# RWKV-6 attention followed by a GELU MLP: the finest level of the attention matrix, taken from TensorE to VectorE

## The chip, the cores and the metric

The kernel runs on one core of one Trainium2 chip. The metric is the device time in microseconds; lower is better. Times given are the median of three runs and one profiled execution, in which a hardware profiler records every instruction.

## The reference, cut to what matters

The first half is a recurrence over 768 steps for 4 batches and 8 heads of 48 channels; its output, laid out as 3072 tokens of 384, goes through an MLP with an exact GELU.

```python
state = np.zeros((B, H, D, D))
for t in range(S):
    cur = einsum('bhd,bhe->bhde', u * k_t, v_t)
    y[:, :, t] = einsum('bhd,bhde->bhe', r_t, state + cur)
    state = w_t[..., None] * state + einsum('bhd,bhe->bhde', k_t, v_t)
x = y.transpose(0, 2, 1, 3).reshape(3072, 384)
h = x @ w_in                       # 384 -> 2048
out = (0.5 * h * (1 + erf(h / sqrt(2)))) @ w_out      # 2048 -> 384
```

So y at step t is a sum over earlier steps s of v_s, weighted by the sum over channels of r_t times the decays w between s and t times k_s; for s = t the factor u stands in place of the decays.

## The kernel before, in words

The sequence is cut into x = 0 to 7, each one half (384 steps) of one batch, all eight heads. `attention(x, unit)` is a generator that computes one x in slots (each `yield` ends one), and `mlp(x)` a generator that computes the MLP of x in steps. The main loop (L844) runs `mlp(x - 1)` and, after its steps, advances `attention(x)` and the first two slots of `attention(x + 1)` at the step numbers in `place` and `place_next`, and starts loads of x + 1 at the step numbers in `times`. There is no scheduler: each engine executes its instructions in the order in which this code issues them, and only waits for what they read or overwrite. Where an instruction on an engine waits, all that was issued to that engine later waits behind it.

In memory channels are on the 128 partitions (two groups g of 64, one per head of a pair) and r, k and w have 1536 steps in the free dimension: four pairs of heads, 384 steps each, step innermost. They lie in two buffers of 4608 floats: `bufs[1]` holds k and w of every x and r of odd x; r of even x has the first third of `bufs[0]`, and the rest of `bufs[0]` holds small things (`alone`, `p1_alone`, `diag_sb`).

Inside chunks of 64 steps the attention matrix `a_sb` is made by levels. For x >= 2 (`quarters`) the levels are h = 1, 4, 16: at level h a block of 4h steps is cut in four, and products between a later quarter of r and an earlier quarter of k are made, where r and k have been multiplied by the decays up to the quarter's edge. At each level VectorE and ScalarE lay out r in `kx` (`lay_out` L442 and L443, `plain` L437), TensorE makes 48 products of 64x64 by 96 columns (L463, a "burst" of 96 records, since each fp32 product is recorded twice), VectorE multiplies r and k by the decays for the next level (L470, L476, L479) and places the results in `a_sb` with nine masked copies (L494). The diagonal s = t is made on VectorE: r k u (L322), summed over 32 partitions by a transposing reduction (L324), then over groups by four small products with a 0/1 matrix `both` (L456), and copied with a mask (L500).

After h = 16, k is transposed by 32x32 blocks (L416), twelve blocks are moved between partitions by transfers (eight on SP's queue, four on ACT's, L411), four copied by ScalarE (L523); then come kv products (L539), the state (L551 to L558), y from `a_sb` (L571), y from the state (L589), and copies and transfers to `xT`, which the MLP reads (L602, L609).

The slots of attention(x), x >= 2: 1 the diagonal's sums; 2 decay totals (L341) and the layout of h = 1; 3 burst h = 1; 4 burst h = 4; 5 burst h = 16; 6 block moves and copies of h = 16; 7 k blocks copied; 8 kv; 9 state; 10 y; 11 y from the state. x = 0 and 1 use another scheme (`halves`), which the change leaves alone.

Steps of `mlp(x)` for x >= 1: 0 to 15 one product group (L656, 384 columns) and its GELU on ScalarE (L659) each, two PSUM buffers in turn; in the groups at f = 13 and 15 VectorE makes sums and differences for a seven-product scheme (L669 to L671); steps 16 to 22 are its seven products of 16 records (L676); odd x (except the last) have two more, 25 steps in all, and even x five more, 28 in all (L760 to L780). `mlp(0)` has 48 steps: 16 groups, then w_out products (L790) while VectorE still converts w_out.

Of the kernel before, what the change touches and what calls it, by code (L numbers as in the profile page):

```python
# [10 lines left out]
F32 = mybir.dt.float32  # L11
# [3 lines left out]
U8 = mybir.dt.uint8  # L15
# [5 lines left out]
C = 64  # L21
# [8 lines left out]
QUARTERS = (1, 4, 16)  # L30
# [13 lines left out]
def kernel(  # L44
# [58 lines left out]
    diag_sb = bufs[0][:, 3 * ALL - NP * T // 32:]  # L103
# [92 lines left out]
    s_qs = {h: q_ints[0][:, i * C:(i + 1) * C] for i, h in enumerate(QUARTERS)}  # L196
# [24 lines left out]
    m_qs = {}  # L221
    for i, h in enumerate(QUARTERS):
        for a in range(3):
            w_q = (3 - a) * C // 4
            z = q_ints[1 if a == 0 else 2]
            o = i * C if a < 2 else i * C + C // 2
            m_qs[h, a] = z[:, o:o + w_q]
            nc.gpsimd.iota(m_qs[h, a], pattern=[[4, C // 4 // h], [0, (3 - a) * h]], base=a, channel_multiplier=0)

    def make_quarter_masks():  # L230
        for (h, a), m_q in m_qs.items():
            nc.vector.tensor_tensor(out=quarter[h][a], in0=s_qs[h][:, 0:m_q.shape[1]], in1=m_q, op=ALU.is_equal)
# [3 lines left out]


    both = const.tile([128, 2, C], F32, name="both")
    nc.gpsimd.memset(both, 0.0)
    for z in range(4):  # L240
        o = slice(z * 32, (z + 1) * 32)
        for i in range(2):
            nc.gpsimd.tensor_copy(out=both[o, z // 2, i * 32:(i + 1) * 32], in_=ident[o, o])
# [55 lines left out]
    def attention(x, unit):  # L299
# [17 lines left out]

        if x >= 2:

            for q in range(qs):  # L320
                z = slice(q * T, (q + 1) * T)
                nc.vector.scalar_tensor_tensor(out=kx[:, z], in0=r[:, z], scalar=u_sb[:, q:q + 1], in1=k[:, z],  # L322
                                               op0=ALU.mult, op1=ALU.mult)
            nc.vector.tensor_reduce(out=diag_sb, in_=kx[:, 0:n_u].rearrange("p (m j) -> p m j", j=32), axis=mybir.AxisListType.X,  # L324
                                    op=ALU.add, apply_transpose=True)
# [17 lines left out]
        if x < 2:  # L343
            yield
# [75 lines left out]
        def quarters():  # L420
# [24 lines left out]
            plain(1)  # L445
            lay_out(1)
            yield
            for h in QUARTERS:
                m, r4, t4, s0, s1, s2 = views(h)
                banks = [ps.tile([128, 2, BANK], F32, name="d", tag="d", bufs=3) for _ in range(0, np_ * NI, 4)]  # L450
                if h == 1:

                    halves_of = diag_sb.rearrange("p (n c z) -> p n c z", c=2, z=2)
                    for g in range(2):
                        for c in range(2):
                            nc.tensor.matmul(banks[-1][half[c], g, 6 * C:6 * C + 2 * np_ * NI], lhsT=both[:, g, :],  # L456
                                             rhs=halves_of[:, :, c], start=True, stop=True)
# [38 lines left out]
                if h == 1:  # L496
                    data = banks[-1][:, :, 6 * C:6 * C + 2 * np_ * NI].rearrange("p g (n z) -> p g n z", z=2)
                    data = data.unsqueeze(4).to_broadcast([128, 2, np_ * NI, 2, C // 2])
                    mask = masks[0].rearrange("p (z t) -> p z t", z=2).unsqueeze(1).unsqueeze(1)
                    nc.vector.copy_predicated(out=at.rearrange("p g n (z t) -> p g n z t", z=2),  # L500
                                              mask=mask.to_broadcast(data.shape), data=data)
# [342 lines left out]
    for x in range(1, NX):  # L844

        place = [1, 2, 4, 7, 9, 11, 13, 15, 17, 20, 24, 32] if x == 1 else [0, 7, 11, 14, 16, 17, 17, 19, 20]
        place_next = [40, 42] if x == 1 else [20, 22]
        loads = load(x + 1, nc.scalar if x > 1 else nc.sync)

        times = range(20, 30) if x == 1 else (2, 3, 4, 5, 15, 16, 17, 19, 20, 21)  # L850
        following = attention(x + 1, 0) if x + 1 < NX else iter(())
        more = iter(())
        for step, _ in enumerate(mlp(x - 1)):
            if x == 1 and step == 2 * NF + 2:
# [79 lines left out]
```

## Time and profile before

| what | value |
|---|---|
| median of three runs | 627.01 us (625.32 to 627.02) |
| profiled execution | 627.31 us, span of its instructions 625.5 us |
| TensorE busy | 607.6 us, 97% of the span |
| VectorE busy | 436.3 us, 70% |
| ScalarE busy | 186.0 us, 30% |
| burst L463, x1728 records | 40.7 us busy |
| masked copies L494, x162 | 82.4 us busy, 550 ns each |
| TensorE clock granted | 0.997 of full over the span |

Busy time is the time in which an engine executed at least one instruction; PE is TensorE, PEld its weight loads, DVE VectorE, ACT ScalarE, POOL GpSimd, SP the queue of transfers. A group of instructions is one line of the code, engine, operation and shape, with its busy time and the mean of one. The chain of waits goes back from the last instruction, at each step to what released it.

### The profile page before, as it was taken

Reading aid. Unit: us, or ns where it says so; the run is one execution under the profiler, and the core shown is the slowest. Engines: PE = TensorE matmul, PEld = TensorE weight load, DVE = VectorE, ACT = ScalarE, POOL = GpSimd, SP = SyncE. Lnnn points to the kernel's source line nnn. Section 1 sums busy time; section 2 is a strip of 40 time slices with the busy share of each in tenths; the row PEclk is TensorE's granted clock in tenths of the full one; section 3 lists DMA queues with packets and bytes.
Section 4 is the critical chain, followed back from the end, with each engine's and each line's share of the span. In section 5 each row is a group of like instructions: output and inputs, shape, how many; then the busy total and the mean of one; then the engine's idle time right before and its main releaser. Section 6 shows DMA issues by size and latency. Waiting matters only on the chain.

```text
span 625.5 us, 16932 instructions
## 1 busy us (share of the span) xinstructions
PE 607.6 (97%) x7462; PEld 456.8 (73%) x7481; DVE 436.3 (70%) x802; ACT 186.0 (30%) x397; POOL 7.6 (1%) x29
## 2 busy tenths in 40 slices
PE   8798999989999999999999999999999999999997
PEld 4565666555689667996689667996689767995694
DVE  8987999798776777668776777677676777340120
ACT  2136556033224222223224232123234233112200
POOL 4000000000000000000000000000000000000000
PEclk9999999999999999999999999999999999999999
DMA  4576348002042214213042113212042002010001
GB/s 158 168 272 253 104 153 291 28 24 89 3 104 74 57 40 90 65 42 89 2 91 88 41 56 73 62 56 83 15 89 87 8 1 39 9 42 7 1 1 38
DMA packets 50505, 46.78 MB, mean 75 GB/s; under 512 B 31616, under 2 KB 35840, under 8 KB 50432
## 3 DMA queue, kind: packets, MB, share of 16 engines
q1 hardware_dynamic: 33120, 29.33, 14.8%
q10 hardware_dynamic: 17312, 16.37, 9.6%
q8 instruction: 59, 0.97, 0.6%
q14 instruction: 14, 0.11, 0.1%
HBM read 36.24 MB, written 4.72 MB: 65 GB/s over the span
## 4 chain that ended last, share of the span: by engine, by line
PE 81%; DVE 12%; issue 3%; DMA 2%; ACT 1%; SPq 0%; DVEq 0%; ACTq 0%
PE h_ps L656 35%; PE o_ps L676 29%; PE d L463 6%; PE o_ps L790 3%; DVE rkw L388 2%; PE d L353 2%; PE y_ps L571 2%; PE y_ps L589 2%; DVE e L291 2%; PE kv_ps L539 2%; DVE a_sb L396 1%; DMA raw<-in_w_in_dram 1%; PE warm L185 1%; DVE w_out_sb L295 1%; DMA xT<-ysb 1%
## 5 line engine op out<-in xcount | busy, mean ns | idle before, releaser
L656 PE MATMUL h_ps<-xT,w_in_sb 128*128 128x384 f32 x768 | 256.6, 491 | 0.4 <-DMA xT<-ysb 0.4
L656 PEld LDWEIGHTS h_ps<-xT,w_in_sb 128*128 128x128 f32 x768 | 144.3, 191 | 96.8 <-ACT xT L602 0.9
L659 ACT ACTIVATE g<-h_ps 128x384 f32<-128x384 f32 (+1 forms) x128 | 57.7, 451 | 216.4 <-PE h_ps L656 200.0
L494 DVE COPY_PREDICATED a_sb<-quarter,d 128x384 f32<-128x384 uint8 x162 | 82.4, 550 | 3.7
L676 PE MATMUL o_ps<-t,s 128*128 128x192 f32 x480 | 82.9, 329 | 0.0
L676 PEld LDWEIGHTS o_ps<-t,s 128*128 128x128 f32 x480 | 78.0, 190 | 0.8
L476 DVE TENSOR_TENSOR rkw<-rkw,tot_sb 128x768 f32<-128x768 f32 x18 | 17.3, 959 | 42.6 <-PE d L463 42.6
L463 PEld LDWEIGHTS d<-kx,rkw 64*64 64x64 f32 x1728 | 37.2, 135 | 9.1 <-issue 7.3
L463 PE MATMUL d<-kx,rkw 64*64 64x96 f32 x1728 | 40.7, 248 | 2.3 <-DVE kx L443 2.3
L790 PE MATMUL o_ps<-w_out_sb,g 128*128 128x384 f32 x128 | 42.7, 490 | 0.0
L437 ACT COPY kx<-rkw 128x384 f32<-128x384 f32 x54 | 31.3, 643 | 29.6 <-PE d L463 21.3
L676 PE MATMUL o_ps<-w_out_sb,g 128*128 128x192 f32 x224 | 39.3, 329 | 0.0
L676 PEld LDWEIGHTS o_ps<-w_out_sb,g 128*128 128x128 f32 x224 | 36.7, 190 | 2.2
L790 PEld LDWEIGHTS o_ps<-w_out_sb,g 128*128 128x128 f32 x128 | 23.9, 190 | 16.1 <-DVE o_sb L796 0.6
L669 DVE TENSOR_TENSOR s<-g 128x512 f32<-128x512 f32 x14 | 9.4, 672 | 29.9 <-ACT g L659 29.9
L676 PE MATMUL o_ps<-t,g 128*128 128x192 f32 x160 | 27.7, 327 | 0.2 <-ACT rkw L661 0.2
L676 PE MATMUL o_ps<-w_out_sb,s 128*128 128x192 f32 x160 | 27.6, 326 | 0.0
L353 PEld LDWEIGHTS d<-rkw 64*64 64x64 f32 x1152 | 18.7, 135 | 11.7 <-issue 5.8
L676 PEld LDWEIGHTS o_ps<-t,g 128*128 128x128 f32 x160 | 26.2, 190 | 0.5 <-ACT rkw L661 0.5
L676 PEld LDWEIGHTS o_ps<-w_out_sb,s 128*128 128x128 f32 x160 | 26.3, 190 | 0.0
L602 ACT COPY xT<-y_ps 48x384 f32<-48x384 f32 x46 | 21.7, 473 | 14.0 <-issue 12.4
L353 PE MATMUL d<-rkw 64*64 64x64 f32 (+1 forms) x1152 | 21.3, 222 | 4.4 <-DVE rkw L388 1.6
(109 smaller groups left out, 591.5 us busy)
## 6 DMA issues: line engine op xcount, KB each, us to landing
rkw<-in_rkw_dram ACTq DMA_DIRECT2D x45, 256.0 KB, 2.8
raw<-in_w_out_dram SPq DMA_DIRECT2D x8, 768.0 KB, 4.4
raw<-in_w_in_dram SPq DMA_DIRECT2D x7, 768.0 KB, 7.5
out_dram<-o_sb SPq DMA_DIRECT2D x21, 192.0 KB, 1.9
v_in<-in_v_dram ACTq DMA_DIRECT2D x5, 584.0 KB, 3.7
rkw<-in_rkw_dram SPq DMA_DIRECT2D x8, 288.0 KB, 3.6
rkw<-in_rkw_dram SPq DMA_DIRECT2D x9, 256.0 KB, 7.5
rkw<-kx SPq DMA_DIRECT2D x48, 48.0 KB, 2.1
```

Source lines behind the costliest of these rows:

```text
L291: nc.vector.scalar_tensor_tensor(out=e, in0=hi, scalar=0x80000000, in1=e, op0=ALU.bitwise_and, op1=ALU.bitwise_or)
L353: nc.tensor.matmul(d[half[p], g, n * width:(n + 1) * width], lhsT=kc[half[g], b, i, p], rhs=right(half[g], b, i, p), start=True, stop=True)
L388: nc.vector.tensor_mul(rk, rk, tt)
L437: nc.scalar.copy(out=z, in_=r4[:, :, :, f, :])
L463: nc.tensor.matmul(d[half[p], g, i * 3 * C // 2:(i + 1) * 3 * C // 2], lhsT=kc[half[g], (n + i) // NI, (n + i) % NI, p], rhs=rx[half[g], 2 ...
L476: nc.vector.tensor_mul(z, z, t2[:, :, 1:2].to_broadcast(z.shape))
L494: nc.vector.copy_predicated(out=an[:, :, :, :, (a + 1) * h:], mask=mask.to_broadcast(data.shape), data=data)
L602: copy(out=xT[s, pair, :].rearrange("p (i c t) -> p c i t", c=2, t=C), in_=y[s])
L656: nc.tensor.matmul(h_ps, lhsT=w_in_sb[:, f // FI, j, f % FI * 128:(f % FI + 1) * 128], rhs=xT[:, j, :], start=(j == 0), stop=(j == NJ - 1))
L659: nc.scalar.activation(out=gs[group][:, f % FG, 0:t], in_=h_ps[:, 0:t], func=AF.Gelu)
L676: nc.tensor.matmul(o, lhsT=lhs(j), rhs=rhs(j), start=start and j == 0, stop=(j == HF - 1), skip_group_check=True)
L790: nc.tensor.matmul(o, lhsT=block(i, f // HF, f % HF), rhs=w_out_sb[:, f, :], start=(f == 0), stop=(f == NF - 1))
```

## The change

The level h = 1 no longer has a burst. For each pair of steps s <= t within a block of four steps, VectorE multiplies r_t by the k_s (with decays) in memory order and writes the results apart, by place in the block (`apart`; for s = t with u as before). The transposing reduction sums each distance e = t - s over 32 partitions into `fine_sb` (`transposed_sums`). Between distances k is multiplied by the decays, and at the end k and r are brought to the state that level h = 4 expects. Eight small products per x with 0/1 matrices `places` sum the remaining partitions and put each result in the row of its step, in the spare columns of the last bank of level h = 4; two masked copies spread them to `a_sb` with `fine_mask`. `both`, `diag_sb` and the h = 1 masks go; `fine_sb` and `places` lie in `bufs[0]`. The first layout is now that of h = 4. There are twelve slots: 1 products with u and their sums; 2 totals, products of the distances and decays of k; 3 their sums and the remaining decays; 4 layout h = 4; 5 small products and burst h = 4; 6 burst h = 16; 7 to 12 as 6 to 11 before. `place`, `place_next` and `times` are changed, for x = 1 too, and the masks and `w_sums` start at step 30 of `mlp(0)` in place of 34.

```diff
...
 N3 = NC // 2
 NI = Q * N3
 LEVELS = (1, 2, 4, 8, 16, 32)
-QUARTERS = (1, 4, 16)
+QUARTERS = (4, 16)
+FINE = 4
 BANK = 512
 PIECE = 768
 AHEAD = 5
...
     ALL = NP * T
     alone = bufs[0][:, ALL:ALL + NF * 128].rearrange("p (f t) -> p f t", f=NF)
     p1_alone = bufs[0][:, ALL + NF * 128:ALL + NF * 128 + DM // 2]
-    diag_sb = bufs[0][:, 3 * ALL - NP * T // 32:]
+    SPARE = ALL + NF * 128 + DM // 2
+
+    fine_sb = bufs[0][:, SPARE:SPARE + FINE * FINE * NPART * NI].rearrange("p (e a n) -> p e a n", e=FINE, a=FINE)
+    places = bufs[0][:, 3 * ALL - FINE * 128:].rearrange("p (a r) -> p a r", a=FINE)
 
     def load_first():
 
...
     row, col, m_h, s_t = (ints[:, i * C:(i + 1) * C] for i in range(4))
 
     q_ints = [wk.tile([128, DM // 2], I32, name=name, bufs=1) for name in ("p1", "u2", "u3")]
-    s_qs = {h: q_ints[0][:, i * C:(i + 1) * C] for i, h in enumerate(QUARTERS)}
+    s_qs = {h: q_ints[0][:, i * C:(i + 1) * C] for i, h in enumerate((1,) + QUARTERS)}
     nc.gpsimd.iota(row, pattern=[[0, C]], base=0, channel_multiplier=1)
     nc.gpsimd.iota(col, pattern=[[1, C]], base=0, channel_multiplier=0)
     nc.vector.tensor_scalar(out=row, in0=row, scalar1=C - 1, scalar2=None, op0=ALU.bitwise_and)
...
 
     quarter = {h: [const.tile([128, (3 - a) * C // 4], U8, name=f"quarter{h}_{a}") for a in range(3)] for h in QUARTERS}
     m_qs = {}
+    t_all, t_block = q_ints[1][:, 2 * C:3 * C], q_ints[2][:, 2 * C:3 * C]
+    nc.gpsimd.iota(t_all, pattern=[[1, C]], base=0, channel_multiplier=0)
+    nc.gpsimd.iota(t_block, pattern=[[1, C // FINE], [0, FINE]], base=0, channel_multiplier=0)
     for i, h in enumerate(QUARTERS):
         for a in range(3):
             w_q = (3 - a) * C // 4
...
             m_qs[h, a] = z[:, o:o + w_q]
             nc.gpsimd.iota(m_qs[h, a], pattern=[[4, C // 4 // h], [0, (3 - a) * h]], base=a, channel_multiplier=0)
 
+
+    fine_mask, later = (const.tile([128, C], U8, name=name) for name in ("fine_mask", "later"))
+
+    def make_fine():
+        nc.vector.tensor_tensor(out=fine_mask, in0=s_qs[FINE], in1=t_block, op=ALU.is_equal)
+        nc.vector.tensor_tensor(out=later, in0=t_all, in1=s_qs[1], op=ALU.is_ge)
+        nc.vector.tensor_tensor(out=fine_mask, in0=fine_mask, in1=later, op=ALU.bitwise_and)
+
+        nc.gpsimd.memset(places, 0.0)
+        for z in range(4):
+            o = slice(z * 32, (z + 1) * 32)
+            v = places[o]
+            v = bass.AP(tensor=v.tensor, offset=v.offset, ap=[v.ap[0], [128 + 1, FINE], [FINE, 32]])
+            nc.gpsimd.tensor_copy(out=v, in_=ident[o, o].unsqueeze(1).to_broadcast([32, FINE, 32]))
+
     def make_quarter_masks():
+        make_fine()
         for (h, a), m_q in m_qs.items():
             nc.vector.tensor_tensor(out=quarter[h][a], in0=s_qs[h][:, 0:m_q.shape[1]], in1=m_q, op=ALU.is_equal)
 
     ident = const.tile([128, 128], F32, name="ident")
     make_identity(nc, ident)
-
-
-    both = const.tile([128, 2, C], F32, name="both")
-    nc.gpsimd.memset(both, 0.0)
-    for z in range(4):
-        o = slice(z * 32, (z + 1) * 32)
-        for i in range(2):
-            nc.gpsimd.tensor_copy(out=both[o, z // 2, i * 32:(i + 1) * 32], in_=ident[o, o])
 
     tot_sb = const.tile([128, NP * T], F32, name="tot_sb")
 
...
             xT_of[x] = wk.tile([128, NJ, T], F32, name="xT")
         xT = xT_of[x]
 
+
+
+        r4, k4, w4 = (z.rearrange("p (m a) -> p m a", a=FINE) for z in (r, k, w))
+        n_m = n_u // FINE
+
+        def transposed_sums(o, e, n):
+            nc.vector.tensor_reduce(out=fine_sb[:, e, 0:n].rearrange("p a n -> p (a n)"),
+                                    in_=kx[:, o:o + n * n_m].rearrange("p (m j) -> p m j", j=32),
+                                    axis=mybir.AxisListType.X, op=ALU.add, apply_transpose=True)
+
+        def apart(e, n):
+
+            o = sum(FINE - i for i in range(1, e)) * n_m
+            nc.vector.tensor_mul(kx[:, o:o + n * n_m].rearrange("p (a m) -> p m a", a=n), k4[:, :, 0:n], r4[:, :, e:e + n])
+            return o
+
         if x >= 2:
-
             for q in range(qs):
-                z = slice(q * T, (q + 1) * T)
-                nc.vector.scalar_tensor_tensor(out=kx[:, z], in0=r[:, z], scalar=u_sb[:, q:q + 1], in1=k[:, z],
+                m_q = slice(q * T // FINE, (q + 1) * T // FINE)
+                nc.vector.scalar_tensor_tensor(out=kx[:, 0:n_u].rearrange("p (a m) -> p m a", a=FINE)[:, m_q],
+                                               in0=r4[:, m_q], scalar=u_sb[:, q:q + 1], in1=k4[:, m_q],
                                                op0=ALU.mult, op1=ALU.mult)
-            nc.vector.tensor_reduce(out=diag_sb, in_=kx[:, 0:n_u].rearrange("p (m j) -> p m j", j=32), axis=mybir.AxisListType.X,
-                                    op=ALU.add, apply_transpose=True)
+            transposed_sums(0, 0, FINE)
             yield
         else:
 
...
             tot[2 * h] = tot_sb[:, at_tot:at_tot + nb]
             nc.vector.tensor_mul(tot[2 * h], t2[:, :, 0], t2[:, :, 1])
             at_tot += nb
-        if x < 2:
+        if x >= 2:
+            def times(z, by):
+                nc.vector.tensor_mul(z, z, by)
+
+            places_of = [apart(1, 3)]
+            times(k4[:, :, 0:2], w4[:, :, 1:3])
+            places_of.append(apart(2, 2))
+            times(k4[:, :, 0:1], w4[:, :, 2:3])
+            places_of.append(apart(3, 1))
+            yield
+            for e, place in enumerate(places_of, 1):
+                transposed_sums(place, e, FINE - e)
+
+            w_01 = tot[2].rearrange("p (m two) -> p m two", two=2)[:, :, 0:1]
+            times(k4[:, :, 0:3], w4[:, :, 3:4].to_broadcast([128, n_m, 3]))
+            times(r4[:, :, 3:4], w4[:, :, 2:3])
+            times(r4[:, :, 1:2], w4[:, :, 0:1])
+            times(r4[:, :, 2:4], w_01.to_broadcast([128, n_m, 2]))
+            yield
+        else:
             yield
 
         def products(bs, right, width):
...
                 nc.vector.tensor_mul(z, r4[:, :, :, 3, :], t4[:, :, :, 2:3].to_broadcast(z.shape))
                 nc.vector.tensor_mul(s0[:, :, :, h:], s1, t4[:, :, :, 1:2].to_broadcast(s1.shape))
 
-            plain(1)
-            lay_out(1)
+            plain(FINE)
+            lay_out(FINE)
             yield
             for h in QUARTERS:
                 m, r4, t4, s0, s1, s2 = views(h)
                 banks = [ps.tile([128, 2, BANK], F32, name="d", tag="d", bufs=3) for _ in range(0, np_ * NI, 4)]
-                if h == 1:
-
-                    halves_of = diag_sb.rearrange("p (n c z) -> p n c z", c=2, z=2)
-                    for g in range(2):
-                        for c in range(2):
-                            nc.tensor.matmul(banks[-1][half[c], g, 6 * C:6 * C + 2 * np_ * NI], lhsT=both[:, g, :],
-                                             rhs=halves_of[:, :, c], start=True, stop=True)
+                if h == FINE:
+
+                    n_b = np_ * NI
+                    fine_ps = [banks[-1][:, g, 6 * C:6 * C + FINE * n_b] for g in range(2)]
+                    for a in range(FINE):
+                        for g in range(2):
+                            nc.tensor.matmul(fine_ps[g][:, a * n_b:], lhsT=places[half[g], a], rhs=fine_sb[half[g], 0:FINE - a, a],
+                                             start=(a == 0), stop=True, skip_group_check=True)
                 ds = []
                 for n, d in zip(range(0, np_ * NI, 4), banks):
                     for i in range(4):
...
                         data = d[:, :, :, o:o + w_q].rearrange("p g n (m x) -> p g n m x", m=m)
                         nc.vector.copy_predicated(out=an[:, :, :, :, (a + 1) * h:], mask=mask.to_broadcast(data.shape), data=data)
                         o += w_q
-                if h == 1:
-                    data = banks[-1][:, :, 6 * C:6 * C + 2 * np_ * NI].rearrange("p g (n z) -> p g n z", z=2)
-                    data = data.unsqueeze(4).to_broadcast([128, 2, np_ * NI, 2, C // 2])
-                    mask = masks[0].rearrange("p (z t) -> p z t", z=2).unsqueeze(1).unsqueeze(1)
-                    nc.vector.copy_predicated(out=at.rearrange("p g n (z t) -> p g n z t", z=2),
-                                              mask=mask.to_broadcast(data.shape), data=data)
+                if h == FINE:
+                    mask = fine_mask.rearrange("p (m b) -> p m b", b=FINE).unsqueeze(1)
+                    for g in range(2):
+                        data = fine_ps[g].rearrange("p (b n) -> p n b", n=n_b)
+                        data = data.unsqueeze(2).to_broadcast([128, n_b, C // FINE, FINE])
+                        nc.vector.copy_predicated(out=at[:, g].rearrange("p n (m b) -> p n m b", b=FINE),
+                                                  mask=mask.to_broadcast(data.shape), data=data)
                 yield
 
         yield from halves() if x < 2 else quarters()
...
 
     for x in range(1, NX):
 
-        place = [1, 2, 4, 7, 9, 11, 13, 15, 17, 20, 24, 32] if x == 1 else [0, 7, 11, 14, 16, 17, 17, 19, 20]
-        place_next = [40, 42] if x == 1 else [20, 22]
+        place = [1, 2, 4, 7, 9, 11, 13, 15, 18, 20, 26, 32] if x == 1 else [1, 6, 8, 13, 15, 16, 18, 18, 20, 21]
+        place_next = [38, 47] if x == 1 else [21, 24] if x % 2 == 0 else [24, 27]
         loads = load(x + 1, nc.scalar if x > 1 else nc.sync)
 
-        times = range(20, 30) if x == 1 else (2, 3, 4, 5, 15, 16, 17, 19, 20, 21)
+        times = range(20, 30) if x == 1 else (2, 3, 4, 5, 16, 17, 18, 19, 20, 21)
         following = attention(x + 1, 0) if x + 1 < NX else iter(())
         more = iter(())
         for step, _ in enumerate(mlp(x - 1)):
-            if x == 1 and step == 2 * NF + 2:
+            if x == 1 and step == 2 * NF - 2:
 
                 make_quarter_masks()
                 more = w_sums()
```

## The prediction

> **What bounds the kernel now.** I read first the share of each engine, then the chain of waits, then busy time by stretches of one mlp each, then groups by shape, then the waits. Part 1 of the page:
>
> ```profile
> PE 607.6 (97%) x7462; PEld 456.8 (73%) x7481; DVE 436.3 (70%) x802; ACT 186.0 (30%) x397; POOL 7.6 (1%) x29
> ```
>
> Stretches, one per mlp from the third on (columns: length, busy PE, PEld, DVE, ACT, POOL):
>
> ```profile
> 204.30:279.10 74.80, 74.80 (x874) 60.02 (x873) 54.93 (x101) 20.36 (x42) 0.00 (x0) 1.00 0.23 60
> 279.10:346.40 67.30, 67.06 (x810) 51.98 (x809) 49.67 (x91) 20.86 (x57) 0.00 (x0) 1.00 0.24 64
> 421.20:488.00 66.80, 66.80 (x809) 52.02 (x809) 49.47 (x91) 20.97 (x57) 0.00 (x0) 1.00 0.25 64
> ```
>
> From 204 us on TensorE has no gap but one of 0.5 us. Whatever leaves TensorE there leaves the time, so long as VectorE, with some 18 to 20 us free per stretch, keeps its deadlines. The chain of waits shows where this doesn't hold, before 141 us, and a stretch where it does:
>
> ```profile
> 128.79 2.13 DVE kx L322 x4
> ...
> 136.18 0.76 DVE kx L442
> 137.03 0.97 DVE kx L443
> 138.13 3.06 PE d L463 x96
> 141.20 14.52 PE h_ps L656 x42
> 155.71 2.14 PE d L463 x96
> ...
> 279.13 1.94 PE h_ps L656 x6
> 281.41 2.14 PE d L463 x96
> 283.55 13.74 PE h_ps L656 x42
> 297.30 2.14 PE d L463 x96
> ```
>
> A burst (96 records, 48 products) costs 2.14 us, an mlp step 1.94. The first fine burst waits 2.3 us for VectorE's layout and then takes 3.06: the granted clock is 0.70 in it and 0.80 in the next 3.8 us.
>
> Groups by shape (busy us, mean ns):
>
> ```profile
> L442 DVE TENSOR_TENSOR kx<-rkw,tot_sb 128x384 f32<-128x384 f32 x12 | 6.6, 552 | 0.0
> L442 DVE TENSOR_TENSOR kx<-rkw 128x384 f32<-128x384 f32 x3 | 2.6, 855 | 0.0
> L364 DVE COPY_PREDICATED a_sb<-mask,d 128x768 f32<-128x768 uint8 x4 | 4.0, 1025 | 0.1
> L324 DVE TRANSPOSE_TENSOR_REDUCE rkw<-kx 128x48 f32<-128x1536 f32 x6 | 10.7, 1778 | 0.2
> ```
>
> The second row is the finest level: both its inputs step 16 bytes, and that costs 855-552 = 303 ns over 384 elements, 0.79 ns each.
>
> **What the Trainium skill says.** "TensorEngine Tiling (Array Packing)", Key Properties: tiles of the array load weights and multiply independently. The trace agrees: 96 records of 64*64, 248 ns each, pass in 2.14 us. "TensorE: Matmul & The Clock Gate", LDWEIGHTS: a load takes columns / 1.2 ns, whatever the rows, so an estimated 107 ns for 128 columns and 53 for 64; the trace's loads last 190 and 135, 55 ns apart for 64 columns. "SBUF — State Buffer" (the passage on cachelines): SBUF lines have 16 bytes and want two hits each, PSUM lines have 8. The 855 against 552 agrees; no row shows VectorE reading PSUM one element per line alone. The Clock Gate page, Part 1: idleness halves the array's clock; the 0.70 agrees.
>
> **The change, part by part.** Attention of x=2 to 7, six times.
>
> TensorE. Gone: the h=1 burst, 2.14, and the four 24-column products that placed the diagonal, 0.35 (280.99 to 281.34): 2.49. New: eight products (16 records) with 64 rows, 128 columns of weights, 12 to 48 columns of data. Loads bound them. Of the old four, pairs of half-width records start 58 ns apart (281.046, 281.103, 281.162 for one half); twice the columns give about 112. If the two row halves overlap, as the 64*64 ones do, 8 pairs x 0.112 = 0.9, with start 1.0. Ends: 0.6 (loads hidden) and 1.8 (16 x 0.112, no overlap). I take 1.0: -1.49 x 6 = **-9.0**.
>
> First transition. h=4 is now the first burst, after step 8, so nothing of mlp(1)'s first steps waits for layouts. From 133.39 to the second burst at 155.71 are 22.3 us, in the loop of x=4 18.17 (279.13 to 297.30): **-4.15** beyond the burst.
>
> mlp(0): attention(1)'s kv goes from step 17 to 18, y from 24 to 26. The waits list has 1.5 us at y for the state and 0.6 at kv for the copied k. VectorE's last w_out conversions end near 114 and 117 and hold the last products, so about **-1.3** of the 2.1 stays. The masks and w sums now fall into VectorE's 3.5 us of idling before 120.6.
>
> The stall near 309.6 (67.25 against 66.77 in the like loop) came from transfers issued on ScalarE ahead of a gelu; they now follow step 15, behind the last gelu: **-0.5**.
>
> ScalarE loses three copies (2.6 us per x), hidden anyway.
>
> VectorE. Gone per x: layouts 0.86+0.96, L470 1.35, L476 and L479 1.92, nine masked copies 6.43 (212.2 to 218.7), L500 1.87: 13.4. New: products 1152/768/384 wide, 1.35+0.96+0.86; k and r multiplies 0.96+0.86, then 1.35+0.86+0.86+0.96; sums of 1152, 768, 384 elements at 1778/1536 ns, 1.33+0.89+0.44; two 768-wide masked copies at L364's 1.03: 13.7. So VectorE stays equal, and what counts is when. Two costs aren't in the trace. (a) 3456 results per x (the four u products, two of the three others) are written 1536 bytes apart. Below: nothing. Above: 2 cycles each, +1.04 ns, since writes of two per line (L479, 959 ns) go at full speed; I take +0.5. (b) The fine copies read PSUM 48 bytes apart: 1.03 to 1.9 us each (L396's 1869 for 768, whose destination steps 8 bytes, as the ceiling). I take 1.2.
>
> Deadlines, with T0 the end of the last mlp's products:
> - Slot 2 starts at T0+0.55: totals 2.6, products and multiplies 5.1; slot 3 (after step 1) 7.0: T0+15.25. ScalarE's three h=4 copies come behind it at step 6 (they queue ahead of the next gelu, due at 15.5, which the PSUM buffers cover); layout h=4 ends at T0+17.2. The burst needs it at 9 x 1.94 + 1.0 = 18.46. Margin 1.26, less 1920 scattered results: none left over at +0.65 ns.
> - Slot 1 (4.0 us) comes at step 24 in the 28-step loops, ahead of the two differences L769 that step 27's product reads two steps (5.2 us) on. Margin 0.2; at +0.5 ns x 1536 it is 0.57 late, in x=3 and 5: **+1.1**. In the other loops L737 has 1.2 to spare.
> - After the h=4 burst VectorE is without a pause: 1.9+1.5+4.0 for h=4, fine copies 2.1, mlp differences 2.0, L470 1.35, L476 and L479 2.0, first transpose 0.6: 15.4. Then eight block moves on SP's queue, 5.8 from first issue to last, 2.3 to land: kv's k is complete 23.5 after the burst's end. TensorE is there after seven steps (13.6), the h=16 burst with its switch (2.3) and three products (7.8): 23.7. Margin 0.2 with copies at 1.03; at my 1.2 it is 0.1 short, six times: **+0.6**. What follows on TensorE (y, the xT copies, the next mlp) waits behind kv.
> - y on the state at step 21: three products, 7.8 us, remain before the next mlp; copies and transfers to xT take 5.1 (260.66 to 265.8). Hidden, 2.7 to spare.
> - SP's and ACT's loads keep their order; k is issued at steps 16 to 18, three steps before slot 1, at 2.8 us to landing. POOL's new memset and four copies run at step 30 of mlp(0), where POOL idles.
>
> Sum: -9.0 -4.15 -1.3 -0.5 +1.1 +0.6 = -13.3. The profiled execution took 627.3 (span 625.5 and 1.8 around it), 0.3 above the median of 627.0: about **613.7**.
>
> **Rivals.**
> - Products that don't overlap: 1.8 instead of 1.0, +4.8 in all: 618. For: no 64*128 tile in the trace. Against: 64*64 tiles overlap fully.
> - The fine copies read at half speed, 1.9 each: transposes, moves and kv come 1.7 later, 1.5 past the margin, so 9.0 in place of 0.6: 622. For: eight-byte lines. Against: in x=0 L396 reads PSUM by 8-byte steps at 1.0 us for 384, no more than its destination alone explains.
> - Slower than before: scattered writes cost what masked copies pay, 0.72 us for 128 elements 16 bytes apart (217.91) against 0.30 contiguous (231.75): +3.3 ns. Slot 2 is then 6.3 later, h=4 5 late per x, slot 1's followers 4 to 5: some 50 us (6.3-1.3 six times, 5 twice, 4 three times, partly at once), 660. The decision falls near +1.6 ns per result (about 2.5 us of stall per x). Against: tensor_tensor writing two per line shows nothing.
> - First two together: about 627, no change.
>
> **How the numbers follow.** Chances: main course 0.62 (its own range 610 to 616.5), no overlap 0.13, slow copies 0.14, scattered writes 0.06, both 0.05. Low end: products at 0.6, no scatter, all of mlp(0)'s waits: 609. High end: the slow copies, 621.5. Some 0.3%, 1.9 us, is what a measurement can tell from no change. Faster takes the first three, less a little: 0.87; same 0.05; slower 0.08.
>
> **What would show it.** The eight products near 1.0 us ahead of the h=4 burst; no gap before mlp(1)'s first burst and no clock below 1.0 there; loops of 73.3 and 65.3 us; the u products at 0.6 to 1.0 us each and the fine copies at 1.0 to 1.4; no TensorE wait at kv for the moves. Wrong if TensorE waits for kx at the h=4 burst or for k at kv, or if the loops don't shrink by 1.5.

## The result, and the profile after

The changed kernel takes 616.93 us in the median of four runs (615.63 to 619.89) against 627.01: the ratio is 0.9852, with a 95% interval of 0.9811 to 0.9893, so it is 1.5% faster. The profiled execution took 617.65 us, its span is 615.7. Forecast were 613.7: the gain is 10.1 us where 13.3 had been worked out.

Part 1 of the page of the kernel after (busy time, share of the span, instructions):

```profile
PE 597.8 (97%) x6934; PEld 448.2 (73%) x6953; DVE 451.0 (73%) x796; ACT 169.8 (28%) x379; POOL 8.4 (1%) x24
```

TensorE has 9.8 us less to do, as wanted. VectorE, forecast equal, has 14.7 us more. The chain of waits of the kernel after (start, duration, engine, work):

```profile
132.87 17.41 PE h_ps L707 x54
150.29 0.99 PE d L506 x16
151.28 2.14 PE d L513 x96
153.43 9.87 PE h_ps L707 x30
...
255.94 8.01 PE o_ps L727 x48
264.34 3.06 DVE kx L352 x4
267.42 1.78 DVE rkw L339
269.20 0.59 DVE s L820
269.92 2.84 PE o_ps L727 x16
...
445.75 4.08 PE h_ps L707 x12
450.29 3.82 DMA rkw<-kx
454.19 0.80 SPq L460
455.03 3.98 DMA rkw<-kx
459.06 1.67 PE kv_ps L590 x92
```

In the first stretch nine mlp steps pass without a gap, then the eight small products (0.99 us) and the burst of h = 4: the wait of 2.3 us and the slow clock that stood here before are gone. In the second, slot 1 of the next attention (the four products with u, then their sums) ends at 269.20, and TensorE waits for the difference behind it. In the third the chain leaves TensorE for the block moves of k: kv can't start before the last of them has landed.

The stretches of one mlp, from its first product to the next one's (columns as before: length, busy PE, PEld, DVE, ACT, POOL, then clock and transfers):

```profile
132.71:198.48 65.77, 65.44 (x721) 50.94 (x720) 52.10 (x90) 18.25 (x54) 0.00 (x0) 1.00 0.26 67
198.48:272.60 74.12, 73.33 (x787) 58.66 (x786) 57.63 (x100) 17.60 (x39) 0.00 (x0) 1.00 0.23 60
413.03:479.64 66.61, 65.42 (x721) 50.89 (x721) 51.90 (x90) 18.28 (x54) 0.00 (x0) 1.00 0.25 66
```

Of the seven stretches of the loop only that of x = 7 is free of a TensorE gap now: in those shown the length exceeds PE's busy time by 0.3 to 1.2 us. By stretches, in us (the last column is the shortest in any version of the changed kernel below, and there without a gap):

| stretch | before | after | without a gap |
|---|---|---|---|
| mlp(0), x = 1 | 85.13 | 83.18 | |
| x = 2 | 70.77 | 65.77 | 65.05 |
| x = 3 | 74.81 | 74.11 | 73.09 |
| x = 4 | 67.26 | 66.32 | 65.05 |
| x = 5 | 74.81 | 74.11 | 73.09 |
| x = 6 | 66.78 | 66.62 | 65.05 |
| x = 7 | 74.78 | 73.09 | 73.09 |
| mlp(1) to the end | 492.14 | 482.96 | 477.36 |

So a stretch without a gap became 1.7 us shorter, a little more than forecast, and 0.72, 1.02, 1.27, 1.02, 1.57 and 0 us of it, 5.60 in all, are lost again. The first product of mlp(0) comes at 48.25 before and 49.53 after; in the versions below it comes anywhere from 47.7 to 50.7, with the loads at the start, and it says nothing of the change.

The waits of the kernel after, for the two places (engine, work, what it waited for: us in all, times, longest):

```profile
PE o_ps L727 <- DVE s L820: 1.6, 2, 0.8
...
PEld kv_ps L590 <- DMA rkw<-kx: 1.3, 1, 1.3
```

The first is slot 1, in x = 3 and 5. The second is one of three waits at kv; the last moves land 0.55, 1.10 and 1.47 us after TensorE has reached kv in x = 2, 4 and 6, and 0.79, 0.73 and 1.71 before it in x = 3, 5 and 7. In the kernel before they landed 2.3 to 2.5 us ahead in every x.

Groups by shape of the kernel after (busy us, mean ns of one):

```profile
L551 DVE COPY_PREDICATED a_sb<-fine_mask,d 128x768 f32<-128x768 uint8 x12 | 11.4, 1006 | 0.2
L352 DVE SCALAR_TENSOR_TENSOR kx<-rkw,u_sb 128x384 f32<-128x384 f32 x12 | 9.1, 880 | 0.0
L346 DVE TENSOR_TENSOR kx<-rkw,rkw 128x1152 f32<-128x1152 f32 x3 | 6.6, 2192 | 0.0
L346 DVE TENSOR_TENSOR kx<-rkw 128x768 f32<-128x768 f32 x3 | 4.6, 1542 | 0.1
```

The fine copies, which read PSUM by steps of 48 bytes, take 1006 ns, as L364 had taken with 1025 for as many elements: that step cost nothing here. The products that are written apart cost more than assumed: 880 ns instead of 611 in memory order, 2192 instead of about 1352.

### The profile page after: what moved, and what is told of

Read it like the earlier page. It is cut to its first block, busy times and chain, and to the rows that moved or that the text cites. A ratio compares the mean times of both kernels' runs of the same rounds, so it can differ in the third digit from the quotient of the medians.

```text
span 615.7 us, 15816 instructions
## 1 busy us (share of the span) xinstructions
PE 597.8 (97%) x6934; PEld 448.2 (73%) x6953; DVE 451.0 (73%) x796; ACT 169.8 (28%) x379; POOL 8.4 (1%) x24
## 4 chain that ended last, share of the span: by engine, by line
PE 81%; DVE 12%; DMA 3%; issue 3%; ACT 1%; SPq 1%; DVEq 0%
PE h_ps L707 37%; PE o_ps L727 27%; PE d L513 4%; PE o_ps L841 4%; DVE rkw L437 2%; DVE e L306 2%; PE d L402 2%; PE y_ps L640 2%; PE kv_ps L590 2%; PE y_ps L622 2%; DVE a_sb L445 1%; DMA rkw<-kx 1%; DVE w_out_sb L310 1%; PE warm L189 1%; DMA raw<-in_w_in_dram 1%
## 5 line engine op out<-in xcount | busy, mean ns | idle before, releaser
L544 DVE COPY_PREDICATED a_sb<-quarter,d 128x384 f32<-128x384 uint8 (+2 forms) x108 | 45.1, 438 | 2.5
L339 DVE TRANSPOSE_TENSOR_REDUCE rkw<-kx 128x48 f32<-128x1536 f32 (+3 forms) x24 | 26.8, 1155 | 0.2
L513 PEld LDWEIGHTS d<-kx,rkw 64*64 64x64 f32 x1152 | 24.3, 133 | 3.4 <-DVE a_sb L551 1.6
L513 PE MATMUL d<-kx,rkw 64*64 64x96 f32 x1152 | 26.5, 245 | 0.0
L607 DVE TENSOR_TENSOR st<-st,kv_ps 128x96 f32<-128x96 f32 x80 | 17.5, 251 | 9.0 <-PE kv_ps L590 7.4
```

Of the source, the lines that this page charges most:

```text
L339: nc.vector.tensor_reduce(out=fine_sb[:, e, 0:n].rearrange("p a n -> p (a n)"), in_=kx[:, o:o + n * n_m].rearrange("p (m j) -> p m j", j=3 ...
L513: nc.tensor.matmul(d[half[p], g, i * 3 * C // 2:(i + 1) * 3 * C // 2], lhsT=kc[half[g], (n + i) // NI, (n + i) % NI, p], rhs=rx[half[g], 2 ...
L544: nc.vector.copy_predicated(out=an[:, :, :, :, (a + 1) * h:], mask=mask.to_broadcast(data.shape), data=data)
L607: nc.vector.tensor_add(z, z, kvs[b][:, :, c // 2, c % 2])
```

## The experiments

Two things were to be explained: the waits at kv in every second x, and the wait at L820. For kv, one block move took much longer than the others in the disturbed passes. The view of the line of the moves in x = 6, kernel after (issue times in ns as minimum, median, maximum; first and last issue; then time from issue to landing):

```profile
L460 SPq DMA_DIRECT2D rkw<-kx x8: 611/628/1714, 448.9 to 455.0; - x8
L460 ACTq DMA_DIRECT2D rkw<-kx x4: 617/638/1952, 450.0 to 453.4; - x4
...
DMA to landing us min/median/max: 2.1/3.6/4.0
```

In x = 5 the same eight go out in 4.9 us, none takes longer than 678 ns to issue, and they land after 2.4 in the median. What the two passes don't share is an entry of the queue of instruction fetches: 16 KB at 451.4, 2.5 us after the first move. The trace has 55 of those in the whole run, each of 0.9 to 1.5 us on one transfer engine. Fetches at 169.1, 310.4 and 451.4 fall among the moves of x = 2, 4 and 6; among those of x = 3, 5 and 7 there is none. 55 blocks of 16 KB are about 0.90 MB; TensorE's records, 6934 and 6953, are 54.2 times 256; the kernel before had 58.4 times 256 of them and 59 entries. The counts fit one entry for each 256 instructions of TensorE.

The kernel before shows a trace of it too. Its stall of 0.5 us in x = 4 comes where ScalarE's queue takes 2.90 us to send out its last three moves, so that the GELUs behind them, and the product that reads them, come late. In x = 6 the same three moves take 2.22 us and TensorE doesn't wait (ScalarE in x = 4, TensorE in x = 4, ScalarE in x = 6):

```profile
316.43 2.90 ACTq L411 DMA_DIRECT2D rkw<-kx  x3
319.69 0.38 ACT L659 ACTIVATE g<-h_ps 128x256 f32<-128x256 f32 x1 [3.58 <-DVE a_sb L494]
...
320.30 2.87 PE L676 MATMUL o_ps<-t,g 128*128 128x192 f32 x16 [0.24 <-ACT rkw L661]
...
458.50 2.22 ACTq L411 DMA_DIRECT2D rkw<-kx  x3
```

A fetch begins at 316.7 in x = 4, 4.4 us after the first move; in x = 6 none falls among the moves.

The theory: a fetch among the moves delays them past kv, so the waits follow the place of the fetches, which depends on how many instructions TensorE has executed. The rival: whatever is fetched, the moves are late where the slots and the loads of k for x + 1 (256 KB each, on ScalarE's queue at steps 16 to 18) put them.

### More instructions ahead

e3_fetch_shift, the kernel after with 40 TensorE instructions more at the start:

```diff
     keep_warm(8)
+    t = ps.tile([128, BANK], F32, name="warm", tag="mm", bufs=2)
+    for _ in range(20):
+        nc.tensor.matmul(t[:, 0:8], lhsT=zeros[:, 0:128], rhs=zeros[:, 0:8], start=True, stop=True)
```

> The changed kernel with 20 products of 8 columns more at the very start, where TensorE waits for the first loads: 40 instructions more on TensorE, nothing else. Theory A (instruction fetches): in the changed kernel the fetches on queue 8 at 169.1, 310.4 and 451.4 us fall among the block moves of x = 2, 4, 6, hold some of them for 1 to 1.5 us, and kv (L590) waits 0.6, 1.0 and 1.4 us for the last. Forty instructions earlier the fetch falls into the burst of h = 16, ahead of the moves; moves land in 2.1 to 2.8 us as in x = 3, 5, 7, kv waits for nothing in x = 2, 4, 6: about 3.0 us faster than the changed kernel, 614. Theory B (the moves compete with each other and with the k loads): nothing moves but noise, the waits at kv stay at 0.6 to 1.4.

Measured: 618.43 us (616.78 to 619.27), ratio to the kernel before 0.9883 [0.9862, 0.9904]. The time expected was wrong, since the fetches landed elsewhere than assumed: 2.8 and 3.9 us after the first move of x = 3 and x = 5, at it in x = 4 and 6, none in x = 2. TensorE now waits at kv in x = 3 (0.93 us) and x = 5 (1.14) and no longer in x = 2; the stretch of x = 4 loses 0.27 us where it lost 1.27, and the moves' lateness in x = 6 went from 1.47 to 0.39. Slots, loads and order were those of the kernel after. The waits went where the fetches went.

e5_fetch_shift_100, the same with `range(50)`, 100 instructions:

> The same with 50 such products: 100 instructions more on TensorE. Theory A: the fetches at 243.4, 383.9 and 523.6 us, which fall into kv of x = 3, 5, 7 in the changed kernel, come some 4 us earlier and so among the last moves of these x; those of x = 2, 4, 6 fall into the h = 16 burst. The waits at kv change sides: none in x = 2, 4, 6, about 0.5 to 1.5 in x = 3, 5, 7. Total near the changed kernel's 617. Theory B: waits stay in x = 2, 4, 6 and out of x = 3, 5, 7.

Measured: 613.06 us (612.22 to 614.56), ratio 0.9803 [0.9782, 0.9825]. Again the fetches came elsewhere than expected: none falls among the moves of x = 2 to 6, and one is 0.7 us after the first of x = 7. The stretches are 65.05, 74.74, 65.05, 74.12, 65.05 and 73.09; of the kv waits 0.23 us in x = 3 is left. From mlp(1) to the end it takes 480.05 us against 482.96, with 100 instructions more to execute; the intervals of the two ratios overlap, so the traces carry this, not the times. Neither run was foretold in its time, but both decide between the theories for the waits that moved: the rival has no reason for a change here. It may hold for the 0.23 us left in x = 3, where no fetch is near.

### The loads of k one step later

e4_loads_later, for what of the rival is left:

```diff
-        times = range(20, 30) if x == 1 else (2, 3, 4, 5, 16, 17, 18, 19, 20, 21)
+        times = range(20, 30) if x == 1 else (2, 3, 4, 5, 17, 18, 19, 20, 21, 22)
```

> The changed kernel with the loads of k and w one step later (17 to 22 for 16 to 21). Theory B: the first k load, issued at 454.1 while the last two moves go out (3.75 and 3.98 us to landing), no longer shares the engines with them, so the waits at kv of 0.6, 1.0 and 1.4 us go: 3.0 faster, 614. Theory A: the fetch still holds the moves; the last two land perhaps 1 us sooner, so the waits shrink but the moves issued before the k load (3.4 to 3.9 us at 450 to 452) stay slow; 0 to 2 us faster.

Measured: 613.27 us (612.53 to 616.12), ratio 0.9813 [0.9785, 0.984], which overlaps that of the kernel after; from mlp(1) to the end 480.21 us against 482.96. Undisturbed moves now land 1.7 us ahead of kv instead of 0.8; a wait is left in x = 4 alone (0.43 us), where a fetch comes 2.0 us after the first move. In x = 6, with one at 3.5, the margin shrinks to 0.2. So the rival holds a part: the first load of k shares the engines with the last moves and takes about 0.9 us of their margin where no fetch falls among them; the fetch takes the rest.

### Slot 1 one step later

e2_slot1_later:

```diff
-        place_next = [38, 47] if x == 1 else [21, 24] if x % 2 == 0 else [24, 27]
+        place_next = [38, 47] if x == 1 else [21, 24] if x % 2 == 0 else [25, 27]
```

> The changed kernel with slot 1 of attention(x + 1) at step 25 in place of 24 in the loops of 28 steps, so behind the differences L820 instead of ahead of them. The four u products and their sum take 4.8 us there and L820 comes 0.8 us too late for the last product in x = 3 and 5. Theory: both stalls go, 1.6 us faster, 615.3, and nothing else moves, since slot 2 begins after step 27 as before. Rival (the 0.8 us belong to L820's other input, the product before): no change.

Measured: 614.58 us (612.7 to 618.12), ratio 0.9815 [0.9789, 0.9841]. The wait at L820 is gone in both stretches, and the one of x = 5 takes 73.09. So the 1.02 us of each long stretch was slot 1. The kv waits stayed and moved a little, 0.32, 0.56, 1.65 and 0.88 us in x = 2, 3, 4 and 6; x = 3 has one now, with a fetch 7.2 us after its first move, behind the issue of the last move and ahead of its landing. The wait in x = 4 cost more than itself: after 1.65 us in which TensorE stood still the granted clock is 0.5 for 3.4 us (320.1 to 323.5), and the stretch takes 68.78. So in this profiled execution, the slowest of the four, the way from mlp(1) to the end is 484.0 us, 1.0 more than in the kernel after, although slot 1 costs nothing in it. The interval of the ratio overlaps that of the kernel after too.

### The writes in memory order

e7_in_order, which writes the outputs of L346 and L352 in memory order:

```diff
-            nc.vector.tensor_mul(kx[:, o:o + n * n_m].rearrange("p (a m) -> p m a", a=n), k4[:, :, 0:n], r4[:, :, e:e + n])
+            nc.vector.tensor_mul(kx[:, o:o + n * n_m].rearrange("p (m a) -> p m a", a=n), k4[:, :, 0:n], r4[:, :, e:e + n])
...
-                nc.vector.scalar_tensor_tensor(out=kx[:, 0:n_u].rearrange("p (a m) -> p m a", a=FINE)[:, m_q],
+                nc.vector.scalar_tensor_tensor(out=kx[:, 0:n_u].rearrange("p (m a) -> p m a", a=FINE)[:, m_q],
```

> The changed kernel with the products of the finest level written in memory order in place of 1536 bytes apart; it leaves out the sorting by place in the block, so the fine sums are of other steps. Theory (scattered writes cost 0.7 ns each): L352 from 880 to 611 ns, L346 1152 wide from 2190 to 1350 and 768 wide from 1535 to 960, 384 wide stays at 855 (its inputs step 16 bytes); slot 1 is 1.1 us shorter, so the waits for L820 in x = 3 and 5 (0.8 each) go: 1.6 faster than the changed kernel; the waits at kv stay. Rival (the cost lies in the strided reads): durations and waits stay.

Measured in one run: 616.57 us. The groups by shape of this run, to be held against those of the kernel after:

```profile
L352 DVE SCALAR_TENSOR_TENSOR kx<-rkw,u_sb 128x384 f32<-128x384 f32 x12 | 6.6, 612 | 0.0
...
L346 DVE TENSOR_TENSOR kx<-rkw,rkw 128x1152 f32<-128x1152 f32 x3 | 4.1, 1351 | 0.0
L346 DVE TENSOR_TENSOR kx<-rkw 128x768 f32<-128x768 f32 x3 | 2.9, 959 | 0.1
```

880 - 612 = 268 ns over 384 results is 0.70 ns each, (2192 - 1351)/1152 is 0.73 and (1542 - 959)/768 is 0.76. VectorE is busy for 437.3 us in this run, 13.7 less than in the kernel after and 1.0 more than in the kernel before: nearly all of its increase of 14.7 was the place of the writes. The waits at L820 are gone here too, without moving slot 1. The kv waits are not (0.26, 0.53, 1.24 and 1.05 us in x = 2, 3, 4 and 6): VectorE's extra time doesn't make them.

### The slots alone, in the kernel before

e1_before_slots puts the new step numbers of mlp(0), as far as the kernel before has these slots, into the kernel before (its second slot of attention(2), with the layout of h = 1, goes to step 41):

```diff
-        place = [1, 2, 4, 7, 9, 11, 13, 15, 17, 20, 24, 32] if x == 1 else [0, 7, 11, 14, 16, 17, 17, 19, 20]
-        place_next = [40, 42] if x == 1 else [20, 22]
+        place = [1, 2, 4, 7, 9, 11, 13, 15, 18, 20, 26, 32] if x == 1 else [0, 7, 11, 14, 16, 17, 17, 19, 20]
+        place_next = [38, 41] if x == 1 else [20, 22]
...
-            if x == 1 and step == 2 * NF + 2:
+            if x == 1 and step == 2 * NF - 2:
```

> The kernel before with only the slots of the first loop changed: kv and y of attention(1) at steps 18 and 26 of mlp(0), masks and w sums from step 30, the first two slots of attention(2) at 38 and 41. The finest level stays on TensorE. Theory: the wait of 2.3 us ahead of mlp(1)'s first burst, the clock drop after it and the waits in mlp(0) go by the slots alone: the loop of x = 2 from 70.8 to 66.6 us, mlp(0) 1 to 2 us shorter, in all 5 faster than before, 622, that is half of the change's gain; the other loops stay at 74.8 and 66.8 to 67.3. Rival (these gains need the new order of levels): 0 to 1.5 faster, the first burst still waits.

Measured: 622.83 us (622.03 to 624.51), ratio 0.9944 [0.9925, 0.9963]. The time is near the 622 expected, the gain is not 5 us but 3.5, since the kernel before took 626.35 beside it. mlp(0) takes 83.72 (85.13 before, 83.18 after), the stretch of x = 2 67.38 (70.77, 65.77); 0.54 us of the 2.3 are left of the gap ahead of its first burst. The stall of x = 4 stands again, with a fetch again 4.4 us after the first move, and costs 0.9 us there in place of 0.5. About 3.5 us of the change's 10 need no new scheme at all, only earlier slots.

### A burst twice

e6_burst_twice makes the products of the h = 4 burst a second time, so as to price a burst on this path:

```diff
-                    for i in range(4):
+                    for i in [0, 1, 2, 3] * (2 if h == FINE else 1):
```

> The changed kernel with every product of the h = 4 burst made twice in place. Theory (TensorE bound, nothing else sets the end): each of six loops grows by a burst, 2.14 us, 12.8 in all, 629.7. Rival (part of TensorE's time is covered by waits for VectorE and transfers): under 10.

Measured in one run: 628.5 us; from mlp(1)'s start to the end 493.92, 10.96 more than the kernel after and less than expected. Stretches without a wait go from 65.05 to 67.07 and from 73.09 to 75.07, so a burst behind another costs 2.0, all of it at the end. Six such bursts would be 12.0; the stretches lose 1.0 us less to waits than in the kernel after. 192 records more per x move the fetches: x = 4 and 6 have none among their moves now and lose 0.27 and 0 us where they lost 1.27 and 1.57, while those of x = 2, 3 and 5 lose 0.2 to 1.0 more than there.

### All three together, and the fetch by itself

e8_best has slot 1 at step 25, the loads a step later and the 50 small products at the start, the edits of e2_slot1_later, e4_loads_later and e5_fetch_shift_100 together.

> The changed kernel with slot 1 of attention(x + 1) at step 25 of the 28-step loops, k and w loads one step later, and 50 small products at the start. Theory: no wait for L820, none or under 0.3 us at kv: loops of 65.05 and 73.1 us, from mlp(1)'s start to the end 477.5 us against 483.0 in the changed kernel's profile: 5 to 6 faster, 611. Rival (the three don't add, since a later slot 1 makes slot 3 or the h = 4 layout late): 613 or more, with a wait at the h = 4 burst.

Measured: 610.37 us in five runs (608.78 to 610.78), ratio to the kernel before 0.9733 [0.9715, 0.975], as expected; its interval, like that of e9_no_shift below, lies wholly below that of the kernel after. Two stretches of e8_best:

```profile
131.36:196.41 65.05, 65.05 (x721) 50.64 (x720) 52.16 (x90) 18.14 (x54) 0.00 (x0) 1.00 0.25 68
196.41:269.50 73.09, 73.09 (x787) 58.68 (x786) 57.56 (x100) 17.49 (x39) 0.00 (x0) 1.00 0.22 59
```

PE is busy for the whole length. From 113.4 us on TensorE has no gap.

e9_no_shift is e8_best without the 50 small products.

> The best version (slot 1 at step 25, loads of k and w one step later) without the 50 small products at the start, so with the instruction fetches where they were. Theory A (a fetch that begins up to some 4 us after the first move holds the moves up): fetches fall about 2 us after the first move of x = 4 and 2.5 to 3.5 after that of x = 6; the last moves there land 1.5 to 2.4 us later than in the other x, kv waits 0.4 to 0.8 us in x = 4 and 0 to 0.3 in x = 6, nowhere else: 0.5 to 1.2 slower than with them. Rival (the 50 products act in another way, or the loads alone cleared kv): no wait at kv in any x.

Measured: 611.85 us (610.44 to 613.31), ratio 0.9769 [0.9743, 0.9796]. Two waits at kv return, 0.49 us in x = 4 and 0.69 in x = 6, exactly where fetches come 2.1 and 2.5 us after the first move; the way from mlp(1) to the end is 479.30 us against 477.36. The intervals of the two ratios overlap, so the traces carry this, not the times. The view of transfers in the 6 us from the first move of x = 6, first in e9_no_shift (the busy share of the 16 transfer engines in forty slices of 0.15 us, in tenths; queue: packets, MB, share of 16 engines; then issues, KB each, median us to landing):

```profile
DMA  0000000058600785988878788311001004899999
...
q8 instruction: 1, 0.02, 1.5%
...
rkw<-kx SPq DMA_DIRECT2D x7, 48.0 KB, 2.5
rkw<-kx ACTq DMA_DIRECT2D x4, 48.0 KB, 3.7
```

and in e8_best:

```profile
DMA  0000000017830388589887898987799999851882
...
rkw<-kx SPq DMA_DIRECT2D x8, 48.0 KB, 2.1
rkw<-kx ACTq DMA_DIRECT2D x4, 48.0 KB, 2.4
```

With one fetch of 16 KB in the stretch only seven of the eight moves of SP's queue have gone out after 6 us, and those of ScalarE's queue land 1.3 us later. The fetch, 447.1 to 448.5, ends where a hole begins: for 1.05 us the engines are busy to 0 or 1 tenth and move 7 to 14 GB/s, and then the moves go on. e8_best has no such hole there. In e9_no_shift the last move lands 0.87 us after TensorE is there, in e8_best 1.75 before.

e10_shift_40 is e8_best with 20 small products, in one run.

> The same with 20 small products at the start in place of 50. Theory A: the fetches fall 2.8 us after the first move of x = 3 and 3.9 after that of x = 5, as with 20 products before; their last moves land 1.5 to 2.4 us later than in x = 7, while x = 2, 4 and 6 land in 7.1 us from the first move on; kv waits 0 to 0.6 us in x = 3 and 5. Rival: all six x alike.

Measured: 610.22 us, 477.36 from mlp(1) to the end, no wait. But the size expected was wrong: fetches 2.5 and 3.6 us after the first move of x = 3 and 5 delayed the last landing by only about 0.6 us, to margins of 1.14 and 1.02.

### All passes together

Six passes (x = 2 to 7) in each of ten versions of the changed kernel, by where a fetch began, time from the first move's issue to the last landing:

| | no fetch | fetch 0 to 0.9 us after the first move | fetch 1 to 6 us after it |
|---|---|---|---|
| a load of k behind the moves | 7.6 to 9.4, median 7.9 (15 passes) | 8.8 to 9.3, 9.2 (5) | 9.4 to 10.5, 9.9 (10) |
| loads a step later, or none (x = 7) | 6.9 to 7.1, 6.9 (18) | 7.0 to 7.8, 7.35 (6) | 7.5 to 9.5, 8.9 (6) |

A fetch in the midst costs 2.0 us in the median, the load of k 1.0. The most that passes without a fetch differ by is 1.8 us, and only where a load is close. Two of the passes counted as without a fetch left TensorE waiting at kv: x = 3 of e5_fetch_shift_100 (9.1 us, 0.23 us of wait), which has none near, and x = 3 of e2_slot1_later (9.4 us, 0.56), where one comes at 7.2 us.

## Why the prediction was right, and where it was wrong

None of the named rivals came, and the time lies in the range, 0.4 us above that of the course forecast as likeliest. But two of the signs that the prediction had named for being wrong came too: TensorE waits for k at kv, and of the loops from x = 3 on only that of x = 7 shrank by 1.5 us (the others by 0.2 to 0.9). The range reached up to 621.5 for slow copies, which did not come; that it held a loss at kv as well was luck. From mlp(1) to the end the steps of the prediction make -12.0 us; measured are -9.2.

- **TensorE's share: right.** The eight products take 0.99 us where 1.0 was taken, so the estimate from "TensorE: Matmul & The Clock Gate", LDWEIGHTS, holds (in one half the loads of 64 columns started 58 ns apart before, those of 128 columns start 112 ns apart now), and the row halves overlap, as "TensorEngine Tiling (Array Packing)", Key Properties, has it. The rival with 1.8 us is out. A stretch shrank by 1.7, not 1.5. The chains account for the 0.2: seven steps behind a burst take 13.74 us, four take 7.94, so 1.93 each and 0.20 more for the first; nine that follow no burst take 17.41, 1.93 each. The sum left out that with one burst less there is one such start less: -1.2 in six.
- **The first transition: right in size.** The stretch of x = 2 without a gap is 65.05, so -4.0 besides the -1.7, where -4.15 was forecast; the gap and the slow clock are gone. e1_before_slots shows that earlier slots bring 3.4 of it in the old scheme.
- **mlp(0):** -1.95 against -1.3, and -1.4 in e1_before_slots.
- **The stall in x = 4:** the stretch without a gap is there as long as the others, so the 0.5 went as forecast. The cause was read in part only: TensorE's gap stands at 320.1, not near 309.6, and the same transfers ahead of a GELU cost nothing in x = 2 and 6. What x = 4 has besides is a fetch, which e1_before_slots repeats.
- **The h = 4 burst: right, with luck.** No wait for `kx` in any x. But by the prediction's own sum nothing of the 1.26 us was left at 0.65 ns for each scattered result, and they cost 0.70 to 0.76. The layout ends 0.5 to 0.75 us ahead of the burst all the same, and 1.95 to 2.2 ahead in e7_in_order: VectorE reaches it some 0.7 us sooner than the sum had it.
- **Fine copies:** 1.0 us instead of 1.2; the rival with 1.9 is out. On PSUM lines the "SBUF — State Buffer" passage states no price for VectorE, and this reading, one value per line, pays none.
- **Scattered writes: the mechanism right, the size off.** The term "+0.5 ns" measured 0.70 to 0.76. So slot 1 cost 1.02 us twice instead of 0.57: 2.0 for 1.1. VectorE, called equal apart from this term, has 14.7 us more, nearly all of it this term. That such writes cost more agrees with the same page's 16-byte lines that want two hits each. e2_slot1_later and e7_in_order both show it, by time and by cost.
- **kv: the step that failed.** It was "eight block moves on SP's queue, 5.8 from first issue to last, 2.3 to land", which left a margin of 0.2 us the same in every x, and 0.6 us of wait in all. The 5.8 was near the time of all twelve moves before (5.5 to 6.1); SP's eight took 4.7 to 5.3. Measured after: 4.9 from first to last and a margin of 0.8 in x = 3 and 5, where no fetch falls among the moves, no margin but 0.55 to 1.47 us of lateness where one does, and 3.6 us lost in x = 2, 4 and 6 (0.72 + 1.27 + 1.57). The fixed times from issue to landing were the fault, with nothing put down for a fetch or for the load of k behind the moves: they were read from passes in which the deadline didn't bind, 2.3 to 2.5 us ahead of kv, where such a delay makes no wait at kv. The change brought the moves and kv closer by 1.7 us, 0.9 of it by the load of k (e4_loads_later), and so a fetch now costs time at kv.

Slot 1 (+0.9), kv (+3.0) and the bursts' starts (-1.2) make +2.7 of the 2.8 us that were missing.

What stays open is a part of how a fetch delays the moves. In the passes with the loads a step later the last move goes out 4.8 to 5.0 us after the first where no fetch is near. With a fetch 1 to 6 us after the first move it went out at 5.45 and 5.53 us in the two passes of e10_shift_40 and landed 2.1 us later. In the four such passes of e4_loads_later and e9_no_shift it went out at 5.7 to 6.2 us, beside a load of k at 6.2, and landed 2.8 to 3.5 us later. So one fetch can cost 0.6 us in one pass and 2.5 in another: it delays the issue by 0.6 to 1.3 us, and where that brings the last move up to the load, landing takes longer as well. No run takes the load away from such a pass, so this second part is argued. The hole behind the fetch in e9_no_shift would fit one engine of sixteen working off its pieces alone (an estimate: a sixteenth of the 130 GB/s ahead of it is 8, and 7 to 14 are moved), but that was not tried by itself. Why the issue is delayed by 0.6 us here and 1.3 there, and what made x = 3 of e5_fetch_shift_100 late, is not known.

## What to carry to other kernels

On the bound engine, work taken away comes back as time only as far as the deadlines around it hold. After the sum of the work, list every small transfer that must land before that engine needs it, and give it the slack that a disturbed pass needs: here a margin of 1.7 us became a lateness of 0.87, so 2.6 us. Issue large loads well behind it. When a wait stands in some passes of a loop and not in others that run the same code, look for what isn't in the code's period, first the queue of instruction fetches.

## What the runs showed of the hardware that was not expected

- Instruction fetches delay data. "Runtime: NRT & Kernel Launch", section "Instruction fetch mechanics", says that a sequencer fetches the next 16 KiB, 256 instructions, over its own queue while it executes, at a cost that is "mostly hidden". The trace agrees with the size (55 entries, 0.90 MB) and, for TensorE's own work, with hidden: in e8_best it has no gap from 113.4 us on. The section doesn't speak of other transfers, and there the cost was not hidden: twelve moves of 48 KB landed 2.0 us later in the median with a fetch among them.
- So the time of this kernel depends on the count of instructions ahead: 40 TensorE instructions more at the start moved the kv waits from x = 2 and 4 to x = 3 and 5, and 100 instead of 40 took all but 0.23 us of them away.
- VectorE paid 0.70 to 0.76 ns for each fp32 result that it wrote 1536 bytes from the last, and nothing for reading PSUM 48 bytes apart (1006 ns for 768 elements under a mask, 1025 for L364 before).
- Once, after 1.65 us without work in e2_slot1_later, TensorE's granted clock was 0.5 for 3.4 us; that cost more than the wait itself (68.78 us for a stretch that takes 65.05 without a gap).
